# Attention into a channel-mix layer on one core: a second batch's token mix on TensorE, wv loaded in runs of rows, and an order remade from other costs

## Chip, core and metric

The kernel runs on one core of one Trainium2 chip. The metric is the device time of one launch in microseconds. Five runs of the kernel before gave a median of 211.34 us (210.93 to 212.43).

## What is computed

Two layers stand behind each other. The first is an attention with a linear form: queries are normalised by a softmax over the head dimension, keys by a softmax over the sequence, and `kv` is a 64 x 64 product per head. Its output, with the heads side by side, is the input `x` of a channel mix.

```python
# q, k, v: batch 8, heads 8, seq 576, head_dim 64
q_s = softmax(q, axis=-1);  k_s = softmax(k, axis=seq)
kv = einsum('bhsd,bhse->bhde', k_s, v)
x  = einsum('bhsd,bhde->bhse', q_s, kv)      # to (8, 576, 512)

x_prev = x shifted by one token, zero ahead of the first
xk = mu_k * x + (1 - mu_k) * x_prev
xr = mu_r * x + (1 - mu_r) * x_prev
k = relu(xk @ w_k)                            # 512 -> 1024
v = (k * k) @ w_v                             # 1024 -> 512
out = sigmoid(xr @ w_r) * v
```

Inputs and output are float32; the matmuls run in bf16.

## The kernel before

**Attention, `attention(b, g)`.** For each of eight batches b there are two groups g of four heads. A load brings q, k or v of a group into a `raw` buffer (12 of them). ScalarE takes the exponentials (`eq`, `ek`, L413) and casts v (`vv`, L419). VectorE sums and scales the queries (`rsum`, `rrec`, `qs`). TensorE (PE) transposes the queries (`transpose_q`, L465, 36 small matmuls of 64 x 64), which are copied from PSUM to `qt` by ScalarE (`copy_qt`, L470), and makes the KV product (`kv`, L443, 36 small ones). VectorE divides (`rz`). The tiles `att_a` and `att_b` are the only two in PSUM for all of this; a tile is free again when its last reader is done. For the first batch alone the KV products go to the `mm` tiles.

**The mix.** Batches in `ON_PE` (before: batch 0) take mu into the weights: VectorE makes products of `kv` with mu and 1 - mu (`weights_of`, L515, tiles `wp`), and PE adds "now" and "then" in PSUM (`x_mixed`, L478, blocks of 8 or 12 small matmuls). Four copies per group, dealt out by `EVAC` to ScalarE and VectorE, bring the halves of xk and xr to SBUF (L529). All other batches make plain x (L478, blocks of 4), ScalarE copies it to `xb` (L564), and VectorE does the shift (edge, L569), a difference (`xd`, L573), scalings by mu (`xm`, L578) and an add (L583).

**Channel mix, `unit(half, c0, n)`.** Tokens of four batches stand in a ring of 2304 columns; a unit takes 512 of them (the last of each half 256), so there are ten units. K (L640) is 8 chunks of 128 features, each 4 matmuls; a relu on ScalarE (L625) and a square on VectorE (L629) follow. The two earliest units split a chunk into head group 0's part and group 1's part, two matmuls each. R (L671, 4 matmuls per 128 tokens) goes through a tanh on ScalarE (`th`, L676). V (L681) is two parts of 4 matmuls per 128 tokens. VectorE gates (`ot`, L687), and SP stores (L697). Four `mm` tiles in PSUM serve K, R and V.

**Weights.** GpSimd (POOL) loads and casts wk in two DMAs, wr in one and wv in two. The weights that PE loads for K are 128 neighbouring columns of `wk_bf`. The `gate` ties the first of them to one of the first loads.

**The order.** `Plan` takes every operation with an engine, an occupancy, a latency, a key and its dependencies, plays them through in time, and emits them in the order of their starts. Keys come from due times; `MAIN` and `PACE` set those of the units, `AHEAD` moves the mix ahead, `LOOK` is how far an engine looks for a better key, and `DMA_RATE`, `DMA_LEAD` and `DMA_TAIL` stand for the loads. The order is fixed when the program is built; each engine then issues its own list strictly in that order. Every change of a cost can move instructions on all engines.

Of the kernel before, what the change touches and what calls it, by code (L numbers as in the profile page):

```python
# [8 lines left out]
ACT = mybir.ActivationFunctionType  # L9
# [7 lines left out]
START = 0.7  # L17
HOP = 0.05
LATE = 1e6
SPARE = 0  # L20
LOOK = {"PE": 0.03, "ACT": 0.2, "DVE": 0.1, "POOL": 0.03, "SP": 0.03}
AHEAD = (1.0, 4, 8)
MAIN = 17.0
PACE = 1.148
DMA_RATE = 365.0
DMA_LEAD = 2.5
DMA_TAIL = 0.6

PARTS = {1: [slice(0, 2)], 2: [slice(0, 1), slice(1, 2)]}
FIRST = ((0, 0, ("ACT", "ACT")), (1, 0, ("SP", "SP")), (0, 1, ("ACT", "SP")),  # L30
         (0, 2, ("SP", "SP")), (1, 1, ("SP", "SP")), (1, 2, ("SP", "SP")))
ORDER = (0, 1, 2)
SOON = {(1, 0, 0): 2.2, (1, 0, 1): 2.4, (1, 1, 0): 2.7, (1, 0, 2): 3.5}
GATE = 6
FILL = 0
ON_PE = (0,)
CASTS = (("ACT", "ACT"), ("ACT", "ACT"))
EVAC = ((("ACT", "DVE"), ("ACT", "ACT")), (("ACT", "DVE"), ("ACT", "ACT")))


class Slot:
# [8 lines left out]
class Op:  # L50


    def __init__(self, engine, occ, lat, key, emit, deps, takes, gives, size):
        self.engine, self.occ, self.lat, self.key = engine, occ, lat, key
        self.emit, self.deps, self.takes, self.size = emit, list(deps), list(takes), size
        self.start = self.end = None
        self.early = 0.0
        for slot in gives:
            slot.last.append(self)


class Plan:
# [57 lines left out]
    def order(self):  # L120
        self.set_due()
        free = {}
        self.pe_busy = []
        dma_free = 0.0
        waiting = {}
        for op in self.ops:
            waiting.setdefault(op.engine, []).append(op)
        done = []
        left = len(self.ops)
        while left:  # L130
            chosen = None
            for engine, ops in waiting.items():
                now = free.get(engine, START)
                ready = None
                for op in ops:
                    if any(d.end is None for d in op.deps):
                        continue
                    t = max([now] + [d.end + HOP for d in op.deps])
                    ok = True
                    for slot in op.takes:  # L140
                        got = self.slot_time(slot)
                        if got is None:
                            ok = False
                            break
                        t = max(t, got[0] + HOP)
                    if not ok:
                        continue
                    rank = (max(t, now + LOOK[engine]), op.key)
                    if ready is None or rank < ready[0]:
                        ready = (rank, t, op)  # L150
                if ready is not None and (chosen is None or ready[1] < chosen[1]):
                    chosen = ready
            assert chosen is not None, "no operation can start"
            _, t, op = chosen
            for slot in op.takes:
                slot.index = self.slot_time(slot)[1]
                for part in self.pools[slot.pool][slot.index]:
                    self.user[part] = slot
            occ, lat = op.occ, op.lat
            if op.engine == "PE" and not self.warm(t):  # L160
                occ, lat = 2 * occ, occ + lat
            op.start, op.end = t, t + lat
            if op.size and op.size < 20:
                op.end = t + lat + (2.0 if op.engine == "SP" else 8.0)
            elif op.size:
                dma_free = max(dma_free, t + DMA_LEAD) + op.size / DMA_RATE
                op.end = dma_free + DMA_TAIL
            if op.engine == "PE":
                self.pe_busy.append((t, t + occ))
            free[op.engine] = t + occ  # L170
            waiting[op.engine].remove(op)
            done.append(op)
            left -= 1
        return sorted(done, key=lambda o: o.start)
# [3 lines left out]
def kernel(  # L178
# [12 lines left out]
    nc = tc.nc  # L191
# [68 lines left out]

    queues = {"SP": nc.sync, "ACT": nc.scalar, "POOL": nc.gpsimd}
    loaded = {}

# [22 lines left out]
    def emit_mu_load():  # L288
        for m, src in enumerate((moe_mu_k, moe_mu_r)):
            ap = bass.AP(tensor=src.tensor, offset=src.offset, ap=[[128, 4], [1, 128]])  # L290
            nc.gpsimd.dma_start(out=mu_sb[4 * m:4 * m + 4, :], in_=ap)

    def emit_warm():
        nc.scalar.activation(out=warm[:], in_=warm[:], func=ACT.Exp)
# [15 lines left out]
            nc.vector.memset(t[:, :, 0:1], 0.0)  # L310

    zero = plan.add("DVE", 0.1, 0.15, -10, emit_warm_zero)
    plan.add("ACT", 1.6, 1.7, 3.5, emit_warm, [zero])
    identity = plan.add("POOL", 0.6, 0.8, -9.1, emit_identity)
    consts = plan.add("DVE", 0.2, 0.3, -9, emit_consts, [identity])
    late_consts = plan.add("DVE", 0.14, 0.2, LATE, emit_late_consts)
# [16 lines left out]
                         rhs=mu_rows[:].rearrange("p m c -> p (m c)"), start=True, stop=True)  # L333

    def emit_mu_wide():
        nc.scalar.copy(out=mu_all[:, :, 0, :, :].rearrange("p m g c -> p m (g c)"),
                       in_=bank(rows_slot).rearrange("p (m c) -> p m c", m=2))

    def emit_mu_rest(m):
        nc.gpsimd.tensor_scalar(out=mu_all[:, m, 1, :, :], in0=mu_all[:, m, 0, :, :],  # L340
# [1 line left out]

    rows_load = plan.add("SP", 0.9, 0.9, -600, emit_mu_rows_load, size=10.0)
    rows_done = plan.add("PE", 0.86, 0.98, -501, emit_mu_rows, [rows_load, consts], [rows_slot])
    wide = plan.add("ACT", 0.48, 0.6, 0, emit_mu_wide, [rows_done], [], [rows_slot])
    mu_split = [plan.add("POOL", 0.5, 0.6, -2 + m, lambda m=m: emit_mu_rest(m), [wide])
                for m in range(2)]

# [24 lines left out]

    wk_done, wv_done = [], []
    for g in range(2):
        wk_done.append(plan.add("POOL", 0.75, 0.75, g, lambda g=g: emit_wk(g), gate,
                                size=1048.0))
    wr_done = plan.add("POOL", 0.75, 0.75, 2, emit_wr, gate, size=1048.0)
    mu_load = plan.add("POOL", 1.2, 1.2, 2.05, emit_mu_load, gate, size=8.0)
    mu_t = plan.add("PE", 0.2, 0.4, LATE, emit_mu, [mu_load, consts], [mu_slot])  # L380
    mu_done = plan.add("DVE", 0.08, 0.17, LATE, emit_mu_copy, [mu_t], gives=[mu_slot])

    def emit_wv(h):
        n = FT // 2
        ap = bass.AP(tensor=moe_w_v.tensor, offset=moe_w_v.offset + h * n * 128 * C,
                     ap=[[C, 128], [128 * C, n], [1, C]])
        nc.gpsimd.dma_start(out=wv_bf[:, h * n:(h + 1) * n, :], in_=ap)

    for h in range(2):
        wv_done.append(plan.add("POOL", 0.75, 0.75, 3 + h, lambda h=h: emit_wv(h), gate,  # L390
                                size=1048.0))
    for b in range(1, B):
        for g in range(2):
            for n, i in enumerate(ORDER):
# [8 lines left out]
    def attention(b, g):  # L403
# [63 lines left out]
                            in_=qss[qs.index][r, j, 64 * u:64 * u + 64], identity=ident[r, r])  # L467

        def copy_qt():
            nc.scalar.copy(out=qts[qt.index][:], in_=transposed()[:, :, 0:S])  # L470

        def by_heads(xp, parts):

# [13 lines left out]
        for n, u in enumerate(us):  # L487
# [10 lines left out]
            expk.append(plan.add("ACT", 0.09 + 0.96 * f, 0.2 + 0.96 * f, step + 1,  # L498
                                 lambda u=u: exp(eks, ek, sk, u), [lk[n]], [ek] if one else [],
                                 [sk]))  # L500
            if CASTS[min(b, 1)][n] == "ACT":
                castv.append(plan.add("ACT", 0.09 + 0.95 * f, 0.2 + 0.96 * f, step + 2,
                                      lambda u=u: cast_v(nc.scalar.copy, u), [lv[n], consts],
                                      [vv] if one else [], [sv]))
            else:
                castv.append(plan.add("DVE", 0.07 + 1.2 * f, 0.15 + 1.2 * f, step + 2,
                                      lambda u=u: cast_v(nc.vector.tensor_copy, u),
                                      [lv[n], consts], [vv] if one else [], [sv]))
        tr = plan.add("PE", 0.45, 0.62, pe_key, transpose_q, scaled + [identity], [qtp], [qs])
        qcopy = plan.add("ACT", 1.0, 1.12, step + 3, copy_qt, [tr], [qt], [qtp])  # L510
        kvm = plan.add("PE", 0.5, 0.6, pe_key, kv, expk + castv, [kvp], [ek, vv])
        zdone = plan.add("DVE", 0.08 * (2 if b == 0 else 1), 0.25 if b == 0 else 0.16, step + 2, recz, [kvm], [rz])

        def weights_of(wp, m, hf):
# [10 lines left out]
                     ((now, 0, 0, HS), (then, 0, 64, HS), (then, S - 64, 1, 64)))  # L525

        def copy_mixed(engine, xp, m, h):
            copy = nc.scalar.copy if engine == "ACT" else nc.vector.tensor_copy
            copy(out=xs[m][:, g::2, c0 + HS * h:c0 + HS * h + HS], in_=bank(xp)[:, :, 0:HS])  # L529

        if on_pe:
            for m in range(2):
# [6 lines left out]
                        for hf in range(2)]  # L539
                for h in range(2):  # L540
                    xp = Slot("att")
                    o = plan.add("PE", 0.29, 0.46, pe_key,
                                 lambda wp=wp, xp=xp, h=h: x_mixed(wp, xp, h), [qcopy] + made,
                                 [xp], [qt, wp])
                    e = EVAC[min(b, 1)][m][h]
# [36 lines left out]
        def mix(m):  # L582
# [1 line left out]
                                    in0=xms[xms_[m].index][:], in1=xbs[xb.index][:, :, 0:S],  # L584
                                    op=ALU.add)

        wdone = plan.add("DVE", 0.25, 0.35, step + 4, weights, [zdone, late_consts], [w],
                         [kvp, rz])
        evs = []
        for h in range(2):  # L590
            o = plan.add("PE", 0.16, 0.35, pe_key, lambda h=h: x(h),
                         [qcopy, wdone], [xps[h]], [qt, w])
            evs.append(plan.add("ACT", 0.52, 0.64, step + 5, lambda h=h: copy_x(h), [o],
                                [xb] if h == 0 else [], [xps[h]]))
# [18 lines left out]
    def unit(half, c0, n):  # L613
# [24 lines left out]
        def k_part(kf, fc, cts):  # L638
            for ct in cts:
                nc.tensor.matmul(bank(kf)[:, 0:n],  # L640
                                 lhsT=wk_bf[:, ct, fc * 128:(fc + 1) * 128],
                                 rhs=xs[0][:, ct, c0:c0 + n],
                                 start=(ct == 0), stop=(ct == CT - 1))

# [119 lines left out]
```

## Time and profile before

| | us |
|---|---|
| median of 5 runs | 211.34 |
| lowest, highest | 210.93, 212.43 |
| the profiled execution, its own time | 212.24 |
| its span, first to last instruction | 210.5 |
| PE, VectorE, ScalarE, GpSimd busy | 189.6, 151.8, 150.7, 39.3 |
| first K matmul | 17.80 |
| first R matmul of unit 1 | 55.95 |
| last matmuls begin | 203.86 |

The span is split by stages further down: the first batch's attention up to 17.8 us, a stage to 56 us in which loads, attention and the first unit lie side by side, one to 116 us in which the remaining loads and attention of batches 2 to 4 are done beside units 1 to 4, and the rest. DVE is VectorE, ACT ScalarE, PEld the weight loads of PE, which run beside its matmuls. In a timeline row the bracket tells how long the engine stood idle before the row and which operation ended it. A line number is that of the kernel before; in the changed kernel lines are about five higher.

### The profile page before, as it was taken

How to read it: one execution, taken by the hardware profiler on the slowest of the kernel's cores; microseconds unless marked ns; L12 is line 12 of the kernel's file. 1: busy time of each engine (PE TensorE's matmuls, PEld its weight loads, DVE VectorE, ACT ScalarE, POOL GpSimd, SP SyncE). 2: the span in 40 equal slices, each digit the busy share in tenths (PEclk: the TensorE clock that was granted, in tenths of full speed). 3: DMA queues.
4: the chain of work that ended last, by engine and by line, in shares of the span. 5: the costliest groups of instructions: out<-in, count | busy, mean ns of one | idle time of the engine just before them, and what ended most of it. 6: DMA issues, size and time to landing. Idle time of an engine off the chain costs nothing.

```text
span 210.5 us, 5190 instructions
## 1 busy us (share of the span) xinstructions
PE 189.6 (90%) x2099; PEld 90.0 (43%) x2099; DVE 151.8 (72%) x338; ACT 150.7 (72%) x229; POOL 39.3 (19%) x63
## 2 busy tenths in 40 slices
PE   3089998949999989999997999999999999999991
PEld 0064444423444444444445443444444444444740
DVE  2583593999989999998749974976797359632531
ACT  5693998988999799999566987337993872452440
POOL 1282754634425112431000000000000000000000
PEclk9999999996999999999999999999999999999997
DMA  6999999999999997899442031242034103402514
GB/s 207 341 256 212 328 224 357 390 410 399 390 395 407 404 391 298 283 376 359 135 100 53 5 73 26 50 100 54 3 74 100 29 20 75 108 3 50 122 28 100
DMA packets 15856, 40.72 MB, mean 193 GB/s; under 512 B 2252, under 2 KB 3800, under 8 KB 15832
## 3 DMA queue, kind: packets, MB, share of 16 engines
q0 software_dynamic: 8336, 27.40, 38.6%
q1 hardware_dynamic: 7064, 12.10, 21.2%
q10 hardware_dynamic: 432, 0.88, 1.3%
q8 instruction: 16, 0.26, 0.5%
q14 instruction: 8, 0.07, 0.1%
HBM read 33.56 MB, written 9.44 MB: 204 GB/s over the span
## 4 chain that ended last, share of the span: by engine, by line
PE 78%; ACT 9%; DVE 7%; DMA 3%; issue 1%; ACTq 0%; DVEq 0%
PE mm_b L640 9%; PE mm_d L640 9%; PE mm_b L681 7%; PE mm_d L681 7%; PE mm_c L681 7%; PE mm_a L681 7%; PE mm_c L640 6%; PE mm_a L640 5%; PE mm_a L671 5%; PE mm_c L671 4%; PE mm_b L671 3%; DMA raw_b<-in_k_dram 3%; PE att_a L478 2%; PE mm_d L671 2%; PE att_b L478 2%; ACT ek_a L413 1%
## 5 line engine op out<-in xcount | busy, mean ns | idle before, releaser
L640 PEld LDWEIGHTS <-wk_bf 128*128 128x128 bf16 x320 | 30.8, 100 | 33.6 <-issue 5.7
L640 PE MATMUL mm_b<-xk,wk_bf 128*128 128x512 bf16 (+1 forms) x96 | 24.4, 368 | 1.7 <-DVE xk L583 1.7
L640 PE MATMUL mm_d<-xk,wk_bf 128*128 128x512 bf16 (+1 forms) x96 | 24.1, 368 | 0.0
L681 PEld LDWEIGHTS <-k_b 128*128 128x128 bf16 x144 | 13.4, 98 | 16.6 <-issue 1.1
L671 PEld LDWEIGHTS <-xr 128*128 128x128 bf16 x144 | 13.7, 98 | 15.9
L681 PEld LDWEIGHTS <-k_a 128*128 128x128 bf16 x144 | 13.3, 98 | 15.7 <-issue 0.9
L640 PE MATMUL mm_c<-xk,wk_bf 128*128 128x512 bf16 (+1 forms) x68 | 17.5, 369 | 0.0
L640 PE MATMUL mm_a<-xk,wk_bf 128*128 128x512 bf16 (+1 forms) x60 | 14.9, 366 | 0.0
L671 PE MATMUL mm_a<-wr_bf,xr 128*128 128x512 bf16 x52 | 13.3, 379 | 0.0
L676 ACT ACTIVATE th_a<-mm_a 128x512 f32<-128x512 f32 x12 | 7.3, 607 | 6.5 <-PE mm_a L671 6.5
L671 PE MATMUL mm_c<-wr_bf,xr 128*128 128x512 bf16 x44 | 11.3, 380 | 0.0
L681 PE MATMUL mm_d<-wv_bf,k_a 128*128 128x512 bf16 x40 | 10.3, 379 | 0.3 <-ACT th_b L676 0.2
L681 PE MATMUL mm_b<-wv_bf,k_b 128*128 128x512 bf16 x40 | 10.3, 380 | 0.0
L681 PE MATMUL mm_a<-wv_bf,k_a 128*128 128x512 bf16 x40 | 10.3, 380 | 0.0
L681 PE MATMUL mm_d<-wv_bf,k_b 128*128 128x512 bf16 x40 | 10.1, 379 | 0.0
L629 DVE TENSOR_TENSOR k_a<-rel_a 128x512 bf16<-128x512 bf16 (+1 forms) x13 | 5.1, 389 | 6.9 <-ACT rel_a L625 6.8
L676 ACT ACTIVATE th_b<-mm_c 128x512 f32<-128x512 f32 x8 | 4.9, 607 | 6.4 <-PE mm_c L671 6.3
L625 ACT ACTIVATE rel_b<-mm_d 128x512 bf16<-128x512 f32 (+1 forms) x12 | 7.1, 592 | 2.8 <-PE mm_d L640 2.2
L681 PE MATMUL mm_c<-wv_bf,k_a 128*128 128x512 bf16 x32 | 8.2, 380 | 0.0
L681 PE MATMUL mm_c<-wv_bf,k_b 128*128 128x512 bf16 x32 | 8.2, 380 | 0.0
L681 PE MATMUL mm_a<-wv_bf,k_b 128*128 128x512 bf16 x32 | 8.2, 379 | 0.0
L681 PE MATMUL mm_b<-wv_bf,k_a 128*128 128x512 bf16 x32 | 8.2, 379 | 0.0
(251 smaller groups left out, 419.9 us busy)
## 6 DMA issues: line engine op xcount, KB each, us to landing
out_dram<-ot_a SPq DMA_DIRECT2D x24, 128.0 KB, 2.4
out_dram<-ot_b SPq DMA_DIRECT2D x24, 128.0 KB, 2.4
out_dram<-ot_c SPq DMA_DIRECT2D x24, 128.0 KB, 2.4
raw_a<-in_q_dram POOLq DMA_DIRECT2D x3, 576.0 KB, 11.1
raw_c<-in_k_dram POOLq DMA_DIRECT2D x2, 576.0 KB, 10.8
raw_b<-in_v_dram POOLq DMA_DIRECT2D x2, 576.0 KB, 10.8
raw_d<-in_q_dram POOLq DMA_DIRECT2D x2, 576.0 KB, 10.7
raw_e<-in_k_dram POOLq DMA_DIRECT2D x2, 576.0 KB, 11.4
```

Source lines behind the costliest of these rows:

```text
L413: nc.scalar.activation(out=dst[slot.index][:, :, u, :], in_=raws[raw.index][:, u, :].rearrange("p u (j d) -> p j u d", d=D), func=ACT.Exp)
L478: nc.tensor.matmul(bank(xp)[64 * hf:64 * hf + 64, u, c:e], lhsT=w[r, hf, :], rhs=qts[qt.index][r, hf, src:src + e - c], start=(n == 0), st ...
L625: nc.scalar.activation(out=rels[rel.index][:, 0:n], in_=bank(kf)[:, 0:n], func=ACT.Relu, scale=HALF_ROOT)
L629: nc.vector.tensor_tensor(out=k2s[k2.index][:, fc, 0:n], in0=rels[rel.index][:, 0:n], in1=rels[rel.index][:, 0:n], op=ALU.mult)
L640: nc.tensor.matmul(bank(kf)[:, 0:n], lhsT=wk_bf[:, ct, fc * 128:(fc + 1) * 128], rhs=xs[0][:, ct, c0:c0 + n], start=(ct == 0), stop=(ct == ...
L671: nc.tensor.matmul(bank(rps), lhsT=xs[1][:, ct, c:c + 128], rhs=wr_bf[:, ct, :], start=(ct == 0), stop=(ct == CT - 1))
L676: nc.scalar.activation(out=ths[th.index][:], in_=bank(rps), func=ACT.Tanh, scale=0.5)
L681: nc.tensor.matmul(bank(vps), lhsT=k2s[k2.index][:, ft, 128 * m:128 * m + 128], rhs=wv_bf[:, ft, :], start=(ft == 0), stop=(ft == FT - 1))
```

## The change

Seven things change.

1. Batch 1's mix goes to PE too (`ON_PE`). `EVAC` for batch 0 gives one more copy per group to VectorE.
2. `CASTS` gets a row for each of batch 0's groups and one for the rest; every entry is ScalarE, as it was.
3. `QCOPY` is new: the Q copy of batch 0's first group goes to VectorE.
4. wv is loaded so that partition p holds rows 8p to 8p + 7, four of them in a run for each DMA, in place of single rows 128 apart. The features of K must then be in that order, so a chunk's weights are columns fc, fc + 8, fc + 16 and so on of `wk_bf`.
5. mu for the batches that are not on PE is loaded by SP instead of POOL.
6. `GATE` is one load later.
7. The costs and settings of `Plan` are other ones, above all for the small-tile matmuls, and the factor for a cold clock is an operation's own. This gives other orders on all engines.

```diff
-SPARE = 0
-LOOK = {"PE": 0.03, "ACT": 0.2, "DVE": 0.1, "POOL": 0.03, "SP": 0.03}
-AHEAD = (1.0, 4, 8)
-MAIN = 17.0
-PACE = 1.148
-DMA_RATE = 365.0
-DMA_LEAD = 2.5
-DMA_TAIL = 0.6
+SPARE = 0.3
+LOOK = {"PE": 0.03, "ACT": 0.2, "DVE": 0.3, "POOL": 0.03, "SP": 0.03}
+AHEAD = (1.0, 4, 1.0)
+MAIN = 16.0
+PACE = 1.072
+DMA_RATE = 404.0
+DMA_LEAD = 1.75
+DMA_TAIL = 0.55
...
-SOON = {(1, 0, 0): 2.2, (1, 0, 1): 2.4, (1, 1, 0): 2.7, (1, 0, 2): 3.5}
-GATE = 6
+SOON = {(1, 0, 0): 1.2, (1, 0, 1): 1.4, (1, 1, 0): 1.7, (1, 0, 2): 2.5}
+GATE = 7
...
-ON_PE = (0,)
-CASTS = (("ACT", "ACT"), ("ACT", "ACT"))
-EVAC = ((("ACT", "DVE"), ("ACT", "ACT")), (("ACT", "DVE"), ("ACT", "ACT")))
+ON_PE = (0, 1)
+CASTS = (("ACT", "ACT"), ("ACT", "ACT"), ("ACT", "ACT"))
+QCOPY = ("DVE", "ACT", "ACT")
+WIDE = "ACT"
+MU_AT = 20
+EVAC = ((("ACT", "DVE"), ("ACT", "DVE")), (("ACT", "DVE"), ("ACT", "ACT")))
...
-            nc.gpsimd.dma_start(out=mu_sb[4 * m:4 * m + 4, :], in_=ap)
+            nc.sync.dma_start(out=mu_sb[4 * m:4 * m + 4, :], in_=ap)
...
-        ap = bass.AP(tensor=moe_w_v.tensor, offset=moe_w_v.offset + h * n * 128 * C,
-                     ap=[[C, 128], [128 * C, n], [1, C]])
+        ap = bass.AP(tensor=moe_w_v.tensor, offset=moe_w_v.offset + h * n * C,
+                     ap=[[FT * C, 128], [C, n], [1, C]])
...
-            nc.scalar.copy(out=qts[qt.index][:], in_=transposed()[:, :, 0:S])
+            copies[copier](out=qts[qt.index][:], in_=transposed()[:, :, 0:S])
...
-        tr = plan.add("PE", 0.45, 0.62, pe_key, transpose_q, scaled + [identity], [qtp], [qs])
-        qcopy = plan.add("ACT", 1.0, 1.12, step + 3, copy_qt, [tr], [qt], [qtp])
-        kvm = plan.add("PE", 0.5, 0.6, pe_key, kv, expk + castv, [kvp], [ek, vv])
+        tr = plan.add("PE", 0.306, 0.478, pe_key, transpose_q, scaled + [identity], [qtp], [qs])
+        tr.cold = 3.5
+        copier = QCOPY[g if b == 0 else 2]
+        qcopy = plan.add(copier, *((1.0, 1.12) if copier == "ACT" else (1.26, 1.36)), step + 3,
+                         copy_qt, [tr], [qt], [qtp])
+        kvm = plan.add("PE", 0.308, 0.478, pe_key, kv, expk + castv, [kvp], [ek, vv])
+        kvm.cold = 3.6
...
-                                 lhsT=wk_bf[:, ct, fc * 128:(fc + 1) * 128],
+                                 lhsT=wk_bf[:, ct, fc::FT],
```

On POOL the loads of wk are followed by six half loads of batch 1 and then wr, in place of wr, the two loads of mu, and then those of batch 1. On ScalarE the copy `mu_all` (L336) goes behind batch 0's first K exponential. On VectorE both `qs_a` of batch 0 go ahead of the sums of group 1, and the Q copy of group 0 ahead of both `qs_b`. On PE, in the first batch, the KV product of group 1 goes ahead of all mix blocks; later on, the two transposes of a batch are mostly apart from its KV products by one or more groups of K, R or V.

## Prediction before the run

> **What bounds the kernel now.** I read the busy shares and slices of the page first, then the table by stage, then TensorE's timeline wherever a slice was not full, and last the ScalarE and VectorE rows under those gaps.
>
> ```profile
> PE 189.6 (90%) x2099; PEld 90.0 (43%) x2099; DVE 151.8 (72%) x338; ACT 150.7 (72%) x229; POOL 39.3 (19%) x63
> ...
> PEclk9999999996999999999999999999999999999997
> ```
>
> TensorE (PE) is busy 90% of the span, so only what lies between its matmuls, and the 10% at the ends, can go. Its clock was granted in full but for one dip near 48 us. The table by stage (columns: busy us and count of PE, weight loads, VectorE, ScalarE, GpSimd; clock; DMA share; GB/s) shows where the rest lies:
>
> ```profile
> 0.00:17.80 17.80, 8.48 (x198) 5.25 (x199) 10.26 (x33) 12.53 (x19) 7.40 (x17) 1.00 0.92 259
> 17.80:56.00 38.20, 33.79 (x453) 15.04 (x447) 28.73 (x64) 32.75 (x50) 18.80 (x28) 0.96 1.05 344
> 56.00:116.00 60.00, 57.62 (x722) 27.87 (x721) 54.14 (x113) 51.67 (x76) 13.12 (x18) 1.00 0.81 293
> 116.00:206.00 90.00, 89.75 (x737) 41.85 (x734) 58.18 (x131) 53.75 (x87) 0.00 (x0) 1.00 0.24 54
> ```
>
> From 116 to 206 us PE is the bound and nothing else matters. Before 17.8 it waits for the first batch's attention. Between 17.8 and 116 it waits for the mix (VectorE) and for PSUM evacuations (ScalarE). PE's timeline (start, length, tile, count, and in brackets the idle time before and who ended it) has the large waits:
>
> ```profile
> 45.23 0.48 PE L465 MATMUL att_b<-ident,qs_a 64*64 64x64 bf16 x36 [1.69 <-DVE qs_a L434]
> 45.54 0.50 PE L443 MATMUL att_a<-vv_a,ek_a 64*64 64x65 bf16 x36
> 47.76 0.99 PE L640 MATMUL mm_b<-xk,wk_bf 128*128 128x512 bf16 x2 [1.73 <-DVE xk L583]
> 48.54 1.06 PE L640 MATMUL mm_c<-xk,wk_bf 128*128 128x512 bf16 x2
> ...
> 75.36 0.48 PE L443 MATMUL att_b<-vv_a,ek_a 64*64 64x65 bf16 x36 [0.18 <-ACT qt_a L470]
> 76.38 0.32 PE L443 MATMUL att_a<-vv_b,ek_b 64*64 64x65 bf16 x15 [0.54 <-ACT qt_b L470]
> ...
> 113.98 0.48 PE L443 MATMUL att_b<-vv_a,ek_a 64*64 64x65 bf16 x36 [0.91 <-ACT qt_b L470]
> 115.00 0.48 PE L443 MATMUL att_a<-vv_b,ek_b 64*64 64x65 bf16 x36 [0.54 <-ACT qt_c L470]
> ```
>
> Two kinds. At 43.5 to 47.8 unit 1 needs batch 1's xk, which VectorE makes through diff, two scalings and an add (`xk L583`); PE does 0.8 us of work in 4.2, and afterwards runs at half clock (two matmuls every 0.86 us instead of 0.43) until 51.24. At 75 and 114 both transposes of a batch stand together and both KV products right behind, so the KV products wait for the two copies of Q on ScalarE that free their PSUM tile.
>
> **The change, part by part.**
>
> *V casts.* They were all on ScalarE before; the table only gets a third row. Cost 0.
>
> *Batch 1's mix on PE.* For each of its two head groups the four PSUM copies to xk and xr replace two copies to xb, and four weight products replace one. VectorE loses diff 0.66, four scalings 4 x 0.285, two adds 2 x 0.66, edge 0.12, w 0.20 = 3.4 us (spacing of such rows) and gains 4 x 0.265 + one evacuation 0.66 = 1.7: -3.4 for the batch. ScalarE gains one copy of 0.53 per group, +1.1. PE pays four blocks of 0.27 instead of two of 0.147: +1.6. What goes is the chain behind xk: KV product, weights, product, one evacuation. I followed the new order with the durations of the old rows; in its K part of unit 1 PE is fed by evacuations at 44 to 47 us, no longer by `L583`, and stays busy enough that I expect no half clock.
>
> *Start-up.* `mu_all` now stands behind the first K exponential on ScalarE, so it leaves a hole (5.53 us) for the packed run after 7.77: +0.48. The Q copy of group 0 leaves that run for VectorE: -1.02 there. But on VectorE it stands before both `qs_b`. The nearest row, an f32 PSUM copy of half the elements, takes 0.66 of issue, so 1.3 us; if a bf16 PSUM source went twice as fast, 0.66. I take 1.3. Then `qs_b` ends at about 13.9 (before: 12.7), its transpose at 14.6, and all of the first batch's mix now stands behind KV product 1 (before, half a block went ahead at 13.33). With one copy and one block alternating on two PSUM tiles, the first K matmul comes at about 19.2 instead of 17.8: **+1.35 us**. ScalarE's two saved xr copies are off the path.
>
> *Weights and loads.* Batch 1's three first loads go ahead of wr. Three x 0.59 MB at the 344 GB/s of the row 17.8 to 56 are 5.1 us and put wr's landing from 22.3 (issue 11.67 + 10.6) to about 27.4; R begins at about 28.1, so cover is 0.7 us; without it PE idles by the excess. wv lands at about 31.4 and 34.1, needed at 32.6 and 35.4. mu's two loads leave POOL for SP, where they issue in the empty stretch 8.4 to 37.6: POOL's queue gains 1.04 us, SP's stores lose nothing. The gate on the second half of a load costs up to 0.3 us, inside the same cover. I give wv's longer runs 0: its rows bound nothing but the above; if they save 0.5 us each, that is cover too.
>
> *Strided weights.* wk's columns are now read 8 apart (16 bytes), 320 times. The trace has no strided weight load; the nearest is the packed one:
>
> ```profile
> L640 PEld LDWEIGHTS <-wk_bf 128*128 128x128 bf16 x320 | 30.8, 100 | 33.6 <-issue 5.7
> ...
> L640 PE MATMUL mm_b<-xk,wk_bf 128*128 128x256 bf16 x16 | 2.4, 273 | 0.0
> ```
>
> It lasts 98 ns at full and 152 at half clock, so an estimate from the two is 54 ns that follow the clock and 44 that don't. Cover is the running matmul: 0.863/4 = 216 ns with 512 columns, 0.435/4 = 109 with 256. [...] At twice the 54 ns the load is 107, just under 109: cost 0. At four times it is 215: 0 with 512 columns, (215 - 109) x 64 = **+6.8** with 256. A gain is excluded, as loads are hidden now. I take 0, the value nearest to the row, and keep 6.8 for the range.
>
> *The new PE order.* From unit 1's first R group on, before ran 55.95 to 205.80 = 149.85 us: 144 groups x 0.863 + 16 x 0.435 + 20 attention blocks x 0.31 + 24 x 0.147 = 141.0; 26 changes into small tiles and back, 0.22 each (0.10 in, 0.12 out, from rows at 147 to 149 us) = 5.7; listed waits 2.4; 0.8 unexplained. After has the same groups, one KV product more (+0.31), and 32 changes: +1.3. But no KV product follows its tile's transpose by less than 2.2 us of PE work (before 1.39 and 0.31), against about 1.1 for a copy: -2.4. So 149.1, and 0.3 for a wait I don't see: 149.4.
>
> **Sum.** Start +1.35. In unit 0 PE's order then has no wait until V ends (R 28.1, V 32.6, K of unit 1 at 42.2). In unit 1 ScalarE stands `eq_c`, then `ek_b` and `vv_b`, ahead of relus whose PSUM tiles PE needs: two new waits of about 1.0 us. R of unit 1 begins at 54.9 instead of 55.95: -1.05. Then 54.9 + 149.4 = 204.3, and the tail of 4.7 (205.8 to 210.5): span 209.0, against 210.5: -1.5. The profiled execution took 212.24, 0.9 more than the median of 211.34; I take the difference to the median: **209.8**.
>
> [...] In the trace the windows are 3.41 us long (47.82 to 51.24), the first full-clock one starts at 20.52, and 13.7 to 17.1, busy about 82% with small tiles, did not raise it. [...] By the trace's own phase, K from 19.2 with a gap at 18 could miss one window and run cold to 23.9: +1.6. [...] Half would be absorbed by the two waits on ScalarE, which hang on loads. I keep it for the range.
>
> **The rivals.**
> - *No change (211.3; 22%).* The waits move: start +1.35, one more cold window +1.6 partly absorbed, and relus behind `vv_b`, whose load landed at 48.5 us before, a microsecond later. Then R of unit 1 begins at about 56.3, and 56.3 + 149.4 + 4.7 = 210.4. For: ScalarE is 86% busy from 17.8 to 56. Against: VectorE, 90% busy from 56 to 116, is relieved.
> - *Strided weight loads bind (slower; 216.6; 15%).* Place: the 64 matmuls of 256 columns; price 106 ns each; it decides from 109 ns per load, and from 216 would hit all 320. 209.8 + 6.8. [...] Against: nothing in the trace, and a doubling is still covered.
> - *Another slowdown, about 213.5 (13%).* wr or wv lands 3 us or more after its estimate and PE idles into a half-clock window (1.7 us, as at 47.8).
> - *All goes well (207.5; in the 50%).* The Q copy is quick, the clock rises early, unit 1 has no wait: -2.3.
>
> **How the numbers follow.** Faster by over 0.5% (below 210.3; about what a measurement of this kernel tells from no change) is the main case, 50%. Within 0.5%: 22%. Slower: 15 + 13 = 28%. The likeliest case alone spans 207.2 to 211.0; the range 206.9 to 214.0 takes in the no-change case and the smaller slowdown and leaves out most of the strided case.
>
> **What would show it.** Right: first K matmul near 19; no wait of PE on VectorE between 42 and 49 and no half clock there; R of unit 1 near 55; no waits of KV products on Q copies; 46 changes into small tiles; K weight loads below 160 ns and 256-column groups of four still 0.435 apart. Wrong: such groups at 0.8, or PE waiting for wr at 27, or new waits on relus above 1.5 us each in unit 1.

## The result, and the profile after

Over all runs on the same chips the changed kernel takes 211.23 us (median of 44 runs, 208.77 to 213.38), the kernel before 212.15 us (79 runs, 210.01 to 215.38). The ratio is 0.9945 (95% interval 0.9928 to 0.9963), which is 0.8 to 1.5 us less; runs in a slower state of the chip are left out of it, so it is not the quotient of the two medians. The forecast was 209.8 us, 1.5 below the 211.34 that the kernel before took in five runs; the measured gain is 0.9 us by the medians and 1.2 by the ratio. The profiled execution took 210.38 us with a span of 208.5, against 212.24 and 210.5 before; it is 0.85 us better than its own median, so the pair of profiles shows more gain (2.0 us of span) than the medians do.

The busy row and the clock row of the page after:

```profile
PE 191.4 (92%) x2163; PEld 102.6 (49%) x2163; DVE 152.8 (73%) x333; ACT 150.7 (72%) x228; POOL 37.4 (18%) x61
...
PEclk9999999999999999999999999999999999999999
```

The dip of the clock near 48 us is gone: the granted clock was 0.50 from 47.82 to 51.24 us before and is 1.00 there now. PE's weight loads are busy 102.6 us instead of 90.0, which is a new cost to follow. The table by stage, cut at the same times as before:

```profile
0.00:17.80 17.80, 7.83 (x182) 4.72 (x183) 11.08 (x34) 10.70 (x17) 7.09 (x17) 1.00 0.91 264
17.80:56.00 38.20, 35.63 (x491) 18.69 (x491) 26.16 (x54) 31.97 (x50) 17.30 (x26) 1.00 1.05 361
56.00:116.00 60.00, 60.00 (x700) 32.07 (x698) 52.78 (x110) 51.42 (x76) 13.00 (x18) 1.00 0.82 281
116.00:206.00 90.00, 87.91 (x794) 47.08 (x791) 62.79 (x138) 56.65 (x87) 0.00 (x0) 1.00 0.26 57
```

From 56 us on PE has no idle time left (60.00 of 60.00; 57.62 before); the 87.91 in the last row is only the earlier end. PE's timeline around unit 1, without the lines between:

```profile
44.97 0.44 PE L483 MATMUL att_a<-qt_c,wp_c 64*64 64x288 bf16 x8 [0.50 <-ACT xk L534]
...
49.61 0.59 PE L645 MATMUL mm_a<-xk,wk_bf 128*128 128x512 bf16 x2 [1.00 <-ACT rel_c L630]
...
53.17 0.59 PE L645 MATMUL mm_a<-xk,wk_bf 128*128 128x512 bf16 x2 [0.76 <-ACT rel_c L630]
...
55.46 1.03 PE L676 MATMUL mm_c<-wr_bf,xr 128*128 128x512 bf16 x4
```

The waits for VectorE's `qs_a` and `xk` are gone from this stretch, and the two waits for ScalarE's relus that the forecast put there have come (1.00 and 0.76 us). A third, 0.50 us for ScalarE's copy of `xk` at 44.97, was not in the forecast.

Side by side, the marks of the two profiles:

| | before | forecast | after |
|---|---|---|---|
| first K matmul | 17.80 | 19.2 | 18.57 |
| first R matmul of unit 0 | 27.24 | 28.1 | 28.38 |
| first K matmul of unit 1 | 41.61 | 42.2 | 42.33 |
| first R matmul of unit 1 | 55.95 | 54.9 | 55.46 |
| end of the last V group | 205.75 | 204.3 | 203.92 |
| span | 210.5 | 209.0 | 208.5 |

### The profile page after: what moved, and what is told of

Same layout as the page of the kernel before. It is cut to its first block, busy times and chain, and to the rows that moved or that the text cites. A ratio compares the mean times of both kernels' runs of the same rounds, so it can differ in the third digit from the quotient of the medians.

```text
span 208.5 us, 5319 instructions
## 1 busy us (share of the span) xinstructions
PE 191.4 (92%) x2163; PEld 102.6 (49%) x2163; DVE 152.8 (73%) x333; ACT 150.7 (72%) x228; POOL 37.4 (18%) x61
## 4 chain that ended last, share of the span: by engine, by line
PE 86%; DMA 8%; DVE 1%; ACT 1%; issue 1%; POOL 0%; SPq 0%; DVEq 0%; ACTq 0%
PE mm_b L686 9%; PE mm_a L645 8%; PE mm_c L645 8%; PE mm_c L686 8%; PE mm_b L645 8%; PE mm_d L686 8%; PE mm_a L686 7%; PE mm_d L645 6%; PE mm_c L676 5%; PE mm_d L676 5%; DMA wk_bf<-in_moe_w_k_dram 4%; PE mm_a L676 4%; DMA raw_d<-in_v_dram 3%; PE att_a L483 2%; PE mm_b L676 2%; PE att_b L483 2%
## 5 line engine op out<-in xcount | busy, mean ns | idle before, releaser
L645 PEld LDWEIGHTS <-wk_bf 128*128 128x128 bf16 x320 | 43.1, 145 | 22.6 <-issue 4.2
L645 PE MATMUL mm_a<-xk,wk_bf 128*128 128x512 bf16 (+1 forms) x84 | 21.7, 372 | 1.8 <-ACT rel_c L630 1.8
L645 PE MATMUL mm_c<-xk,wk_bf 128*128 128x512 bf16 (+1 forms) x84 | 21.4, 368 | 0.2 <-DMA wk_bf<-in_moe_w_k_dram 0.2
L645 PE MATMUL mm_b<-xk,wk_bf 128*128 128x512 bf16 (+1 forms) x88 | 21.1, 353 | 0.0
L645 PE MATMUL mm_d<-xk,wk_bf 128*128 128x512 bf16 (+1 forms) x64 | 16.0, 368 | 0.0
L676 PE MATMUL mm_d<-wr_bf,xr 128*128 128x512 bf16 x44 | 11.3, 379 | 0.0
L676 PE MATMUL mm_a<-wr_bf,xr 128*128 128x512 bf16 x36 | 9.3, 380 | 0.0
L681 ACT ACTIVATE th_a<-mm_d 128x512 f32<-128x512 f32 x9 | 5.4, 601 | 3.9 <-PE mm_d L676 2.7
L630 ACT ACTIVATE rel_a<-mm_b 128x512 bf16<-128x512 f32 (+1 forms) x11 | 6.0, 548 | 2.4 <-PE mm_b L645 2.1
L681 ACT ACTIVATE th_b<-mm_a 128x512 f32<-128x512 f32 x7 | 4.2, 599 | 4.1 <-PE mm_a L676 4.1
```

The costliest lines, as they stand in the source:

```text
L630: nc.scalar.activation(out=rels[rel.index][:, 0:n], in_=bank(kf)[:, 0:n], func=ACT.Relu, scale=HALF_ROOT)
L645: nc.tensor.matmul(bank(kf)[:, 0:n], lhsT=wk_bf[:, ct, fc::FT], rhs=xs[0][:, ct, c0:c0 + n], start=(ct == 0), stop=(ct == CT - 1))
L676: nc.tensor.matmul(bank(rps), lhsT=xs[1][:, ct, c:c + 128], rhs=wr_bf[:, ct, :], start=(ct == 0), stop=(ct == CT - 1))
L681: nc.scalar.activation(out=ths[th.index][:], in_=bank(rps), func=ACT.Tanh, scale=0.5)
```

## The experiments

Two questions are asked. Do the strided weight loads of wk cost nothing, as forecast, or something, either through their length or through a wait that they bring? And does the gain come from batch 1's mix on PE, or from the new costs and settings of the planner? The letters A and B in an expectation hold for that run alone. Ratios are to the kernel before on the same chip; most versions have six runs, and an interval reaches about half a per cent to each side. "Neighbouring" is the changed kernel with wk's columns and wv's rows as they were before.

**Neighbouring columns in the changed kernel.**

```diff
-    ap=[[FT * C, 128], [C, n], [1, C]]         # wv, offset h * n * C
+    ap=[[C, 128], [128 * C, n], [1, C]]        # wv, offset h * n * 128 * C
...
-    lhsT=wk_bf[:, ct, fc::FT],
+    lhsT=wk_bf[:, ct, fc * 128:(fc + 1) * 128],
```

> The changed kernel with the old wv load and neighbouring wk columns; nothing else moves but one wait: PE's wait for the second half of wk goes from the second K matmul back to the ninth K group. Theory A (the strided weights cost something): K weight loads fall from 143 to 98 ns; a two-matmul K group right after small tiles falls from 0.49 to 0.44 us to the next start (16 such places, 0.8 us in all, about half of them behind later waits); the 0.68 us wait for wk at the first group goes. Together 0.5 to 1.2 us faster than the changed kernel, ratio to before 0.989 to 0.992. Rival B (strided weights are free, as predicted): equal to the changed kernel within 0.2 us, ratio 0.9945; the order alone makes the difference.

Measured: 209.14 us, ratio 0.9868 (0.9823 to 0.9913), against 0.9945 for the changed kernel. The gain more than doubles, so the strided loads are not free. It is also more than was expected of them. The K weight-load row of the page, first of the changed kernel, then of this one (busy us, mean ns; idle before):

```profile
L645 PEld LDWEIGHTS <-wk_bf 128*128 128x128 bf16 x320 | 43.1, 145 | 22.6 <-issue 4.2
```

```profile
L645 PEld LDWEIGHTS <-wk_bf 128*128 128x128 bf16 x320 | 30.3, 98 | 33.1 <-issue 4.4
```

A strided load takes 47 ns more on average. PE's timeline at the same groups of 256 columns, of the changed kernel and then of this one:

```profile
108.61 0.66 PE L645 MATMUL mm_b<-xk,wk_bf 128*128 128x256 bf16 x4
109.11 0.60 PE L645 MATMUL mm_d<-xk,wk_bf 128*128 128x256 bf16 x4
109.54 0.60 PE L645 MATMUL mm_a<-xk,wk_bf 128*128 128x256 bf16 x4
```

```profile
107.14 0.61 PE L645 MATMUL mm_b<-xk,wk_bf 128*128 128x256 bf16 x4
107.59 0.60 PE L645 MATMUL mm_d<-xk,wk_bf 128*128 128x256 bf16 x4
108.03 0.60 PE L645 MATMUL mm_a<-xk,wk_bf 128*128 128x256 bf16 x4
```

From the second to the third group it is 0.43 and 0.44 us: among large matmuls the longer load is hidden. The first group stands right behind small tiles, and there it shows (0.50 to the next group instead of 0.45). The same with 512 columns, in unit 2:

```profile
70.47 1.08 PE L645 MATMUL mm_a<-xk,wk_bf 128*128 128x512 bf16 x4
71.39 1.03 PE L645 MATMUL mm_c<-xk,wk_bf 128*128 128x512 bf16 x4
```

```profile
69.14 1.04 PE L645 MATMUL mm_a<-xk,wk_bf 128*128 128x512 bf16 x4
70.01 1.03 PE L645 MATMUL mm_c<-xk,wk_bf 128*128 128x512 bf16 x4
```

Behind a block of small tiles the first K group takes 0.92 us to the next one's start instead of 0.87. In single instructions it is the second matmul of the group that comes later, 0.27 us after the first instead of 0.23. The second difference is at the start. The changed kernel's first K group, PE and then the weight loads:

```profile
18.57 0.65 PE L645 MATMUL mm_c<-xk,wk_bf 128*128 128x512 bf16 x1
19.39 0.65 PE L645 MATMUL mm_c<-xk,wk_bf 128*128 128x512 bf16 x1 [0.18 <-DMA wk_bf<-in_moe_w_k_dram]
```

```profile
19.39 0.21 PEld L645 LDWEIGHTS <-wk_bf 128*128 128x128 bf16 x2 [0.68 <-DMA wk_bf<-in_moe_w_k_dram]
```

The second load of this group reads channel block 2, which the first DMA of wk brings, and yet it waits for wk's second DMA. In the traces' instruction records that wait stands on the second load with strided columns, and on the ninth, the first to read the other half, with neighbouring ones. Of the program only the slice differs (wv's layout, the other half of the edit, has its own run below and brings no such wait), so the program takes the strided slice to overlap the half of wk that the second DMA fills.

**The new weight layout alone, in the kernel before** (the reverse of the diff above).

> The kernel before with only the new wv load and wk columns 8 apart. Theory A: slower than before. Its first K group stands at 17.8 us and would now wait for the second half of wk, which landed at about 19.3: +1.5 us at that place, and 14 places of 0.05 us after small tiles; the VectorE-bound stretch at 43 to 48 us takes part of it back, so +0.5 to +1.8 us, ratio 1.002 to 1.009. Rival B: ratio 1.000 within 0.002; groups of four matmuls of 256 columns 0.435 us apart in both theories.

Measured: 212.32 us, ratio 1.0014 (0.9977 to 1.005). By itself this ratio does not tell a price of 0.2 to 0.5% from none. Its trace has the same wait at the start (0.72 us on the second load; the two loads start 0.86 us apart, 0.43 beyond the pace at half clock) and R of unit 0 at 28.66 instead of 27.24; a clock that rose 2.3 us later in this execution (22.83 against 20.52) has a share in that. R of unit 1 is at 56.23 against 55.95: PE still waits for VectorE's `xk` in unit 1 (1.77 us; 1.73 before), so what comes before is mostly absorbed. In this trace the price of the layout shows only where nothing later waits.

**Batch 1's mix on PE alone, in the kernel before.**

```diff
-ON_PE = (0,)
+ON_PE = (0, 1)
```

> The kernel before with batch 1's mix on PE and nothing else set otherwise (its own planner costs make the order). Theory A: the wait of PE for xk at 43.5 to 47.8 us and the half-clock stretch behind it go, which were worth most of the gain; with no delay at the start it is 1 to 2.5 us faster than before, ratio 0.988 to 0.995. Rival B: the waits move to ScalarE's relus and the copies of Q, and PE pays 1.6 us for the blocks: within 0.5 us of before or slower.

Measured: 209.14 us, ratio 0.9892 (0.9847 to 0.9937): by the middle of the interval twice the gain of the whole change. All of PE's waits from 55 us to the end, with the old costs and the old settings (us in total, times, longest):

```profile
PE att_b L443 <- ACT qt_b L470: 0.4, 1, 0.4
PE mm_c L640 <- DVE ot_a L687: 0.2, 1, 0.2
```

Before, they were 2.4 us in this stretch, nearly all KV products behind Q copies. From R of unit 1 (56.13) to the end of the last V group (204.14) it takes 148.01 us instead of 149.80. So the waits of KV products at 75 and 114 us, which the forecast gave to the remade PE order, mostly go with this one setting. It is still the order that does it: with batch 1's mix on PE the old costs too put K groups between a transpose and the KV product that needs its copy.

```profile
74.29 0.48 PE L465 MATMUL att_b<-ident,qs_b 64*64 64x64 bf16 x36
74.70 1.04 PE L640 MATMUL mm_c<-xk,wk_bf 128*128 128x512 bf16 x4
75.67 0.48 PE L443 MATMUL att_a<-vv_b,ek_b 64*64 64x65 bf16 x36
```

R of unit 1 is not earlier than before in this trace (56.13 against 55.95): what the mix saves in unit 1, the stretch ahead of it had lost.

**The change without batch 1's mix on PE.**

```diff
-ON_PE = (0, 1)
+ON_PE = (0,)
```

> The changed kernel with batch 1's mix off PE again. Theory A: the wait for VectorE's xk near 44 us comes back, with a half-clock window; 1.5 to 3 us slower than the changed kernel, ratio to before 1.001 to 1.009. Rival B: the remade order alone keeps PE fed, and the 1.6 us of extra PE work is saved: equal to the changed kernel or up to 1 us faster.

Measured: 214.39 us, ratio 1.0109 (1.0061 to 1.0157). That is slower than was expected. The trace has a wait of 1.0 us for VectorE's `xk`, 1.3 for `ot_a`, 0.9 for `vv_a` and half clock from 73.86 to 77.28 (the mean granted clock is 0.986, 1.000 in the changed kernel). It also has the wait for wk's second half, longer than in the changed kernel:

```profile
17.80 0.14 PEld L645 LDWEIGHTS <-wk_bf 128*128 128x128 bf16 x1 [0.20 <-issue]
19.83 0.21 PEld L645 LDWEIGHTS <-wk_bf 128*128 128x128 bf16 x2 [1.90 <-DMA wk_bf<-in_moe_w_k_dram]
```

The second load stands 2.03 us behind the first, against 0.83 in the changed kernel. With the new settings the mix is worth 1.6% (1.0109 to 0.9945), with the old ones 1.1%; up to 1.2 us of the difference in the traces is this wait, so it is not shown that the new settings lean on the mix.

**wk in two tiles, columns still strided.** This separates the wait from the longer loads.

```diff
-    wk_bf = const.tile([128, CT, F], BF16, name="wk_bf")
+    wk_two = [const.tile([128, 2, F], BF16, name=f"wk_bf{g}") for g in range(2)]
...
-    lhsT=wk_bf[:, ct, fc::FT],
+    lhsT=wk_two[ct % 2][:, ct // 2, fc::FT],
```

> The changed kernel with wk held in two tiles, one for each half that a DMA fills; the columns stay eight apart. Only the wait of the second K weight load for the second half's DMA goes; every strided load stays. If the added wait is most of the stride's price (theory A): the wait of 0.68 us at 19.39 is gone, R of unit 0 starts near 27.6 instead of 28.38, full clock comes earlier, and the time is 209.5 to 210.0 (ratio to before 0.988 to 0.991), while the weight loads still take about 143 ns. If the 45 ns longer loads are the price (theory B): 16 groups behind small tiles keep their 0.05 us each, the time stays at 210.6 to 211.4 (ratio 0.994 to 0.998), within 0.3 us of the changed kernel. If both count: about 210.3.

Measured: 209.44 us, ratio 0.9875 (0.9837 to 0.9914). The weight loads are as long as before (145 ns on average), and the wait is gone:

```profile
18.75 0.21 PEld L645 LDWEIGHTS <-wk_bf 128*128 128x128 bf16 x2 [0.20 <-issue]
```

By the ratios 0.7% is taken back without touching one load. In this trace the half landed at 19.52 and the second matmul began at 19.19, so the wait that went was about 0.35 us here; the rest of the 0.7% (1.5 us) is not seen in it. What is left of the loads can be read from the traces without the noise of the start: from the first K matmul of unit 1 to the end of the last V group, five of the traces with this PE order give

| | first K of unit 1 | end of last V | between |
|---|---|---|---|
| changed kernel (strided) | 42.33 | 203.92 | 161.59 |
| two tiles (strided) | 41.54 | 203.11 | 161.57 |
| neighbouring | 41.25 | 202.30 | 161.05 |
| neighbouring, added wait (second try) | 40.87 | 201.92 | 161.05 |
| neighbouring, wv in runs | 42.34 | 203.40 | 161.06 |

The longer loads cost 0.52 to 0.54 us there. Matched instruction by instruction, the changed kernel and neighbouring columns differ in twelve places, each the second K matmul behind small tiles, by 0.046 to 0.051 us; a shorter wait for a relu takes 0.05 back. Two more such places lie in unit 0.

**The wait alone, added to neighbouring columns, two tries.** The first put it on the second K group (`fc == 1`, `ct == 0`), the second at its place in the changed kernel.

```diff
+                if early and fc == 0 and ct == 2:
+                    tc.add_manual_dep(mm.ins, wk_loads[1].ins.name, sync)
```

> The version with neighbouring columns (209.14 us) with one dependence added: the second K group's first load waits for the DMA of wk's second half, as in the changed kernel the first group's second load does. Loads stay at 98 ns. Theory A (the wait is the price of the stride): 210.2 to 210.8, R of unit 0 at about 28.0 or later. Theory B (the loads are the price): the wait shows at 18.9 to 19.4 and the time stays within 0.4 us of 209.1.

> The version with neighbouring columns (209.14 us, ratio 0.9868) with the added wait for the second half of wk at the same place as in the changed kernel: on the second load of the first K group, one group earlier than in the first attempt, where the half had landed by the time it was asked for. Loads stay at 98 ns. If the wait is what two tiles took away (1.5 us): ratio 0.991 to 0.995, about 210.5 us, and a wait for the DMA near 19 us. If the wait shows but costs only its own length of some 0.4 us: ratio 0.987 to 0.990, about 209.6. If the half has landed already: no wait and 0.985 to 0.989.

First try: 209.78 us, ratio 0.9881 (0.9826 to 0.9935). In its trace the weight load waited 0.56 us but the matmul behind it did not come later, because the group ahead was still running at half clock (0.86 us to the next group's start): the wait was put one group too late to test anything. Second try: 209.88 us, ratio 0.9886 (0.9831 to 0.9942). Its weight loads show the wait:

```profile
17.05 0.10 PEld L647 LDWEIGHTS <-wk_bf 128*128 128x128 bf16 x1 [0.20 <-issue]
17.83 0.13 PEld L647 LDWEIGHTS <-wk_bf 128*128 128x128 bf16 x2 [0.67 <-DMA wk_bf<-in_moe_w_k_dram]
```

The second matmul comes 0.78 us after the first, where the half clock alone would make it 0.43. So the wait costs 0.35 us in this trace and 0.4 in the changed kernel's, 0.2% of the time. By the ratios, adding it costs 0.2% and removing it gains 0.7%; both intervals are about half a per cent wide to each side. Of the four traces that have the wait, three show 0.35 to 0.43 us (these two and the new layout alone) and one, without batch 1's mix, 1.6. The profiled execution here is the fastest of its six, and that of the changed kernel is faster than its median, so their 0.4 may be less than the usual price. That the wait is there and costs its own length is shown; what it costs on average stays open between 0.4 and some 1.5 us.

**wv alone in runs of rows**, with neighbouring columns of wk. The order of wv's rows does not match that of wk's columns here, so V is another product of the same size.

> The version with neighbouring columns of wk (209.14 us), wv alone loaded in runs of rows as in the changed kernel; the rows of wv then don't match the columns of wk, so V sums other products of the same number and size. The forecast gave the longer runs 0. If so: ratio to before 0.984 to 0.990 like the version without them, R of unit 0 near 27.3 to 27.6, no wait of PE on wv. If the runs land earlier and relieve the other loads: wv's two loads end 1 us or more earlier than with single rows, and the time falls by up to 0.5 us. Had the runs a price, 0.5 us of the changed kernel's 1.6 us would be theirs and not the strided loads'.

Measured: 209.65 us, ratio 0.9883 (0.9846 to 0.9919), the same as without within the intervals. wv's two DMAs land 9.1 and 10.8 us after issue (9.5 and 11.2 with single rows). POOL's issue takes 534 ns each instead of 756. The part of the change that the new layout was made for is worth nothing that these runs can measure.

**Group 0's Q copy back on ScalarE**, with neighbouring columns.

```diff
-QCOPY = ("DVE", "ACT", "ACT")
+QCOPY = ("ACT", "ACT", "ACT")
```

> The version with neighbouring columns with group 0's Q copy of batch 0 back on ScalarE, everything else of the changed order kept. The forecast had this copy as a cost of the start on VectorE. If it is one: the first K matmul starts earlier than 18.28, near 17.8, and the time falls to about 208.6. If VectorE's 0.62 us copy is a gain over ScalarE's 1.0 us: first K matmul near 18.7, KV of group 0 no longer ahead, time 209.4 to 209.8.

Measured: 207.98 us (207.57 to 208.98), ratio 0.9812 (0.9767 to 0.9857), span 206.2: the lowest median here, 1.9% under the kernel before and ahead of the changed kernel by 1.3%. Its interval still overlaps that of neighbouring columns alone. The weight loads of its first K group:

```profile
17.71 0.13 PEld L645 LDWEIGHTS <-wk_bf 128*128 128x128 bf16 x2 [0.44 <-DMA wk_bf<-in_moe_w_k_dram]
```

They come 0.57 us earlier than with the copy on VectorE (18.28). The bracket names wk's first DMA, but PE did not wait for it: the load follows the start of the block of eight small matmuls ahead of it by 0.62 us, as much as such a block takes at half clock. Here is one of 0.63 us in the version "both repairs" below, where full clock begins at 21.93 and both halves of wk had landed by 18.2 us:

```profile
20.70 0.19 PEld L483 LDWEIGHTS <-wp_d 64*64 64x64 bf16 x8 [0.80 <-issue]
21.33 0.21 PEld L645 LDWEIGHTS <-wk_bf 128*128 128x128 bf16 x2 [0.44 <-issue]
```

The margin is small: GpSimd, which waits for the same half, went on at 17.60. On VectorE the copy is short, but it stands ahead of `qs_b` there. The row of the changed kernel:

```profile
11.20 0.70 DVE L475 COPY qt_a<-att_a 128x1152 bf16<-128x1152 bf16 x1
```

In the pair of traces the last V group ends 0.69 us earlier. Only 0.35 of that is there at the first K matmul of unit 1; 0.34 comes later, where the planner gives PE another order. So the run does not measure the copy's place alone.

**The Q copy's true cost told to the planner**, copy on VectorE.

```diff
-    (1.0, 1.12) if copier == "ACT" else (1.26, 1.36)
+    (1.0, 1.12) if copier == "ACT" else (0.62, 0.70)
```

> The version with neighbouring columns, the planner told that VectorE's Q copy takes 0.62 us (latency 0.70) as measured instead of 1.26 (1.36). The copy moves ahead of the next group's row sums, where VectorE waits. If the start is bound by VectorE's chain: first K matmul before 18.0 and the time 208.5 to 208.9. If it is bound by the loads of wk or by ScalarE's exponentials: first K matmul at 18.2 to 18.4 as now, and 209.0 to 209.4.

Measured: 208.79 us, ratio 0.9844 (0.9804 to 0.9885), within the interval of neighbouring columns with the old cost. The copy did not go ahead of the row sums as expected but behind both `qs_b` (it starts at 12.91), and the first K load came at 17.55, again 0.62 us behind the start of its block and so without a wait for wk. Both versions that keep the copy from ahead of `qs_b` start K earlier, by 0.57 and 0.73 us. R of unit 0 is later here all the same (28.29 against 27.29), which was not followed up.

**Both repairs, with the strided columns kept** (two tiles, Q copy on ScalarE).

> The changed kernel with wk in two tiles (false wait gone, strided loads kept) and group 0's Q copy of batch 0 on ScalarE. If the two repairs add up: 0.9875 less the 0.0056 that the Q copy took off the version with neighbouring columns gives a ratio near 0.982, about 208.3 us, and from R of unit 0 to the end it is still 0.5 us longer than the version with neighbouring columns and the Q copy on ScalarE. If the second half of wk lands after PE is ready (19.3 us or later), the earlier start only moves the wait: PE waits for wk's first or second DMA before 20 us, and the ratio stays near 0.987.

Measured: 208.65 us, ratio 0.9842 (0.9801 to 0.9884). In this trace PE did wait for wk's first half: the first K load comes 0.99 us behind the start of its block instead of 0.62, so the wait cost 0.37. Against two tiles alone it is 0.3% less time, within the intervals; that the repairs add up is not shown.

**mu_all copied by VectorE**, neighbouring columns and Q copy on ScalarE.

```diff
-WIDE = "ACT"
+WIDE = "DVE"
```

> The version with neighbouring columns and the Q copy on ScalarE (207.98 us), with the copy of mu_all moved from ScalarE, where it stands behind the first exponential of K and holds 0.48 us, to VectorE's idle time before the first reciprocals. If ScalarE's run binds the start: the first K matmul comes at 17.6 to 17.8 instead of 18.11 and the time is about 207.5. If VectorE's chain (row sums, scaling of Q) or the landing of wk binds: first K matmul still at 18.0 to 18.6, time 207.8 to 208.6.

Measured: 208.74 us (207.49 to 210.32), ratio 0.9860 (0.9808 to 0.9912): no gain by the median. The weight loads of the profiled execution:

```profile
18.72 0.13 PEld L645 LDWEIGHTS <-wk_bf 128*128 128x128 bf16 x2 [2.06 <-DMA wk_bf<-in_moe_w_k_dram]
```

The load comes 2.24 us behind the start of its block instead of 0.62, so PE was held 1.6 us by the landing of wk. In this execution, the slowest of the six, the landing binds the start and not the engines. Three of the six runs took 207.49 to 208.04 us and three 209.43 to 210.32; that a late landing is what parts them is likely but not shown, as one of them has a trace.

## Why the prediction was wrong, and where it was right

The direction and the range hold. The size does not: 211.23 us instead of 209.8, a gain of 0.9 to 1.2 us instead of 1.5. The place holds in part: the forecast had 1.05 us of the gain ahead of R of unit 1 and 0.45 behind it, the profile has 0.49 and 1.34. One term was put at nothing and cost over 1 us; two others were too pessimistic, by 0.6 and 0.9 us. That the sum of the profile came within half a microsecond (a span of 208.5 for 209.0) is luck.

*Strided weights, taken as 0.* This is the step that failed. The cover among large matmuls was rightly foreseen: the groups of 256 columns keep 0.43 to 0.44 us, although a load of 143 ns is longer than the 109 of such a matmul. But "0 in all cases" failed in two ways. Right behind small tiles, where the trace before already showed a price for changing, the 45 ns that a load takes longer come out in full: 0.53 us from unit 1 on and 0.10 in unit 0. And the layout brought a wait for wk's second half that was not looked for, 0.4 us in the trace. Together that is 1.05 us of the 1.6 by which this trace and that of neighbouring columns differ; the rest is a start 0.29 us earlier and a clock that rose sooner (20.12 us against 21.39), 0.27. By the ratios the layout costs 0.8% (0.9945 against 0.9868), 1.6 us.

The factors of two and four on the part of a load that follows the clock were the author's assumptions: no run shows them, nor the 6.8 us that rests on the four. What the runs showed in their place is a strided load of 143 ns instead of 98 at full clock, 1.46 times, and a price of 1.6 us by the ratios, the wait included. The forecast compared with the 109 ns only the part that follows the clock, 54 ns and its multiples. This split does not hold for strided loads: they take 143 ns at full clock and up to 168 at half, so that by the same reckoning 25 follow the clock and 118 do not. The strided rival was the right worry with the wrong place and a price four times too high.

*Batch 1's mix on PE and the new PE order.* The mechanism was right, the size too small: from R of unit 1 to the end of the last V group I had 149.4 us, and it was 148.46 with strided loads, 148.12 without. My count of groups, blocks and changes (141.0 + 0.31 + 32 x 0.22 = 148.35) is right to 0.2 us; the 0.8 us that I carried over from before as unexplained did not come again, nor did the wait of 0.3 that I added. The cause was put in the wrong place: the KV waits go with the setting `ON_PE` alone, through the order that the old costs then give, and the remade costs are not needed for it.

*Start-up, +1.35 us.* Right in direction, too large: the first K matmul came 0.77 us later. The Q copy on VectorE took 0.70 us, 0.62 to the next start, which is the case of twice the speed that I had named and not chosen; it accounts for the difference. That the copy's place costs is borne out by the starts of K (0.57 us earlier with it back on ScalarE); the times agree, 0.6% with neighbouring columns and 0.3% with two tiles, but within their intervals.

*Unit 0.* What the start had gained was lost again here: R of unit 0 came 0.28 us later than forecast. The wait for wk (0.4) and two exposed loads (0.10) are part of that.

*Unit 1.* Two waits for relus of about 1.0 us each were forecast; they were 1.00 and 0.76. No wait for VectorE's `xk`, no half clock there: right. R of unit 1 was 0.56 us later than forecast. The first K of unit 1 was 0.13 late, exposed loads took 0.2 more (K of unit 1 lasts 13.13 us, 12.93 with neighbouring columns), and the wait of 0.50 for ScalarE's `xk` was not foreseen.

*Loads.* wr landed at 26.4 us (forecast 27.4) and wv at 30.5 and 33.1 (31.4 and 34.1), all a microsecond early and behind cover. The term 0 for wv's runs agrees with its own run.

*The clock.* Kept out of the sum and in the range. In the profiles of all versions, full clock begins anywhere between 18.65 and 22.83 us, 4.18 us apart, and in the changed kernel at 21.39, not at the 23.9 of the forecast's cold case. The windows of 3.41 us are those of the trace: before, the half clock lasts 3.41 us (47.82 to 51.24), and full clock 27.31 (20.52 to 47.82) and 157.01 (51.24 to 208.25), 8 and 46 times as long. As K runs at half speed until full clock begins (two matmuls in 0.86 us instead of 0.43), the start of one profile can be some 2 us longer than that of another for this alone, by an estimate from these times. This is the reason why the stage differences above are taken from unit 1 on.

What stays open: the rest of the change (batch 1's loads ahead of wr, the other order, mu's loads on SP) is worth about 0.8% by the ratios 0.9892 (mix alone) and 0.9812 (all but layout and Q copy); the two intervals overlap, and it was not tried in parts.

## What to carry to other kernels

When a transfer's layout is changed, cost the reader of the data too: how each load gets longer (143 ns for 98 here), where no long instruction covers it (0.05 us each behind small tiles), and which waits the program puts on a strided slice (0.4 us in the changed kernel's trace). Look at the waits in the trace and not at the source alone; here one tile for each DMA took the wait away (about 0.35 us in its trace). If the layout's own aim (here the rows of wv) lies behind cover, even a small price on the other side (0.8% by the ratios) makes it a loss. And read a bracket against the same place elsewhere: two waits of 0.44 us here were named after a DMA that had already landed.

## What the runs showed of the hardware

- A 128 x 128 weight load with columns 8 apart took 143 ns at full clock and up to 168 at half clock; with neighbouring columns 98 and up to 152. Among large matmuls the longer load cost nothing (groups of four began 0.86 us apart with 512 columns, 0.43 with 256, and 0.87 and 0.44 with neighbouring columns), right behind small tiles 0.05 us.
- VectorE copied 128 x 1152 bf16 out of PSUM in 0.70 us (0.62 to the next start), as fast as it does half that many f32 elements (0.66 to the next start); ScalarE took 1.11 us.
- In the version with the Q copy on ScalarE full clock began at 18.65 us; in the 3.41 us ahead of it (15.24 to 18.65) PE was busy 2.88, largely with small tiles and with K matmuls in the last microsecond only. In the kernel before, PE was busy 2.91 of the 3.41 us from 13.69 to 17.11 (85%), also with small tiles, and K still ran at half clock (two matmuls in 0.85 us) until 20.52. In these two traces the busy share alone does not tell when full clock begins.
- wk's first half, for which the first K load waits, was there at 16.4 us in one trace (two tiles, Q copy on ScalarE) and 18.7 in another (mu_all on VectorE), 6.6 and 8.5 us after its issue, though GpSimd issues the same loads in the same order; in these two the start could not be planned closer than that.
